# A row transform folded twice, a new order of steps, and norm steps kept in accumulator columns

## The chip, the core and the metric

The kernel runs on one core of one Trainium2 chip. The metric is the device time of one execution in microseconds (us), as the median of several runs. The core has a matrix engine (TensorE, PE in the rows), a vector engine (VectorE, DVE), a scalar engine (ScalarE, ACT), GpSimd (POOL) and a DMA queue on SyncE (SP). Results of TensorE land in PSUM, everything else lies in SBUF.

## The reference

Three parts in a row: a decayed linear attention over blocks, a mixer that adds the real part of a two-dimensional Fourier transform and then a normalised feed-forward block, and a gated convolution with two projections.

```python
def _moe_ref(x, w_ch1, w_ch2):            # x: (2, 768, 512), the attention's output
    X = np.fft.fft(x, axis=1)             # over the 768 rows
    X = np.fft.fft(X, axis=2)             # over the 512 features
    u = x + np.real(X)
    mu = np.mean(u, axis=-1, keepdims=True)
    var = np.mean((u - mu) ** 2, axis=-1, keepdims=True)
    un = (u - mu) / np.sqrt(var + 1e-06)
    return u + np.maximum(un @ w_ch1, 0.0) @ w_ch2      # 512 -> 2048 -> 512
```

Ahead of it, for 8 heads of 64 features and blocks of rows: `intra = (q k^T * decay) v`, `inter = (q * power) state`, and the state is decayed and gets `k^T v`. Behind it: `gate = sigmoid(causal 5-tap convolution of x)`, `out = (gate * (x w_val)) w_out`.

## The kernel before, in words

**Layout.** Everything between attention and output is held transposed: U of each batch is 128 partitions x 4 feature tiles x 768 rows. The features are ordered so that tiles 2 and 3 hold the mirror of tiles 0 and 1, so that a transform can work on sums and differences of tiles.

**Attention.** Twelve chunks of 128 rows (two batches of six). Names of its steps in the order table: L loads a chunk, S the scores (L242), s the masked scores on VectorE (L248), A scores times values (L257), T and t the state update (L295, L303), E the state's share (L268), Kq the scaled query (L216), Y the state's decay, k the scaled keys on ScalarE (L228), a, e and r the copies into U.

**Transform, per batch.** fft_pm (Xm, L311) makes sums and differences of the feature tiles, 768 wide. fft_fold (Xo, L322) folds row s with row 768 - s, plus for the cosine half (w = 0) and minus for the sine half (w = 1), so 384 rows remain; row 384 is taken apart in fft_a384 (XA, L337). First step, fft_D (XD, L350): the folded rows are the stationary side, in three blocks of 128 rows, and the feature tables `cd` are streamed, 257 or 256 columns; fft_Dev (Xd, L359) copies the result to AB. Second step, fft_P and fft_Q (L375, L365): a group of three matmuls, AB blocks against the row tables `cos` and `sin`, 385 columns each, one group for each half of the features (g). An fp32 matmul stands as two records in the trace, so a group has six. fft_qev (Xq) and fft_pc (Xc, L381) evict, fft_mp (Xp, L385) adds and subtracts cosine and sine results, u_add (Xu, L500) adds that to U. fft_P256 (XK, L401) and fft_fix (XF) do feature frequency 256 in two half-array tiles.

**Norm.** ln_mean (Nm, L521) sums U over features with matmuls; ln_center (Nc, L528) subtracts; ln_square and ln_var give the variance in a PSUM tile; ln_newton (Nw, L557 to L566) makes 1/sqrt with eight tiny VectorE operations of 3 columns, in an SBUF tile `var`.

**Feed-forward.** Four blocks of 384 rows, 16 hidden chunks each. F is the first matmul (L627 in block 0, eight records a chunk; L619 to L621 in the others), f and h the relu and its remainder, G the second matmul, U/u and V/v the split of weights into two parts, on ScalarE and then on VectorE or GpSimd. Weights come as 64-bit numbers, in units of 1024 KB, and are converted by bit operations: Da, Dx on ScalarE, Db (L472), Dc (L481), De (L485) on VectorE. Three raw buffers are shared by the units, so a load waits for the conversion three units back.

**What sets the order.** A hand-written table, ORDER: 1454 tokens, run through once. Each engine gets its instructions in the order of the tokens and works through them one by one. A `+` behind a token puts it on VectorE instead of GpSimd (or ScalarE). PSUM tiles of the transform, the norms and the gate share one pool of two buffers.

## Time and profile before

| | |
|---|---|
| median of 3 runs | 447.0 us (445.47 to 447.66) |
| profiled execution | 447.84 us, span 446.1 us |
| TensorE busy | 436.8 us (98%), 2750 records |
| VectorE busy | 314.8 us (71%) |
| ScalarE busy | 248.4 us (56%) |
| GpSimd busy | 114.8 us (26%) |
| DMA | 38.88 MB, most of it in the first 170 us |

The span is what the profiler saw between first and last instruction; the execution's own time is 1.7 us longer. A busy matrix engine is not one at its peak, since records overlap: what counts is the distance from one record's start to the next.

### The profile page before, as it was taken

What the parts mean: (1) busy time and instruction counts of PE and PEld (TensorE: products, weight loads), DVE (VectorE), ACT (ScalarE), POOL (GpSimd) and SP (SyncE); (2) the same over time, 40 slices, a digit from 0 to 9 for tenths busy, and PEclk for the clock granted to TensorE, in tenths of its full rate; (3) what the DMA queues carried; (4) which work ended last, traced back from release to release, by engine and by line L of the source; (5) the groups of instructions that cost most, each with busy time, mean ns of one, the idle gap of its engine ahead of it and who ended that gap; (6) DMA issues with size and microseconds to landing.
All of it is one profiled execution on the core that took longest, in us unless ns stands there. A gap on an engine that the chain in (4) does not pass through costs nothing.

```text
span 446.1 us, 7062 instructions
## 1 busy us (share of the span) xinstructions
PE 436.8 (98%) x2750; PEld 391.9 (88%) x2750; DVE 314.8 (71%) x519; ACT 248.4 (56%) x507; POOL 114.8 (26%) x102
## 2 busy tenths in 40 slices
PE   8999998999999999999999999999999999999996
PEld 6888765876777789999999999999999999999995
DVE  5878997999898989978863677525726883330494
ACT  5576772777667765785436466434635743341442
POOL 2221251021343012136027142122233032331210
PEclk9999998999999999999999999999999999999999
DMA  7899922338634530000000000000000010000101
GB/s 267 301 312 392 396 96 94 101 150 281 225 116 167 168 118 1 1 1 1 0 1 24 0 1 25 0 2 24 0 1 1 24 47 1 0 1 24 49 1 71
DMA packets 14465, 38.88 MB, mean 87 GB/s; under 512 B 1632, under 2 KB 2656, under 8 KB 13408
## 3 DMA queue, kind: packets, MB, share of 16 engines
q1 hardware_dynamic: 14144, 38.04, 23.9%
q8 instruction: 21, 0.34, 0.3%
q10 hardware_dynamic: 288, 0.39, 0.3%
q14 instruction: 12, 0.10, 0.1%
HBM read 35.29 MB, written 3.15 MB: 86 GB/s over the span
## 4 chain that ended last, share of the span: by engine, by line
PE 80%; DVE 3%; ACT 0%; issue 0%
PE acc L619 10%; PE acc L621 10%; PE acc L620 10%; PE ph L627 8%; PE ph L619 8%; PE ph L621 7%; PE ph L620 7%; PE pso L619 4%; PE pso L621 4%; PE pso L620 4%; PE pso L350 1%; PE pso L521 1%; PE pso L550 1%; PE pso L375 1%; PE pso L365 1%; DVE gate L714 1%
## 5 line engine op out<-in xcount | busy, mean ns | idle before, releaser
L619 PE MATMUL acc<-g,w2s 128*128 128x384 f32 x240 | 84.7, 353 | 0.0
L620 PE MATMUL acc<-g,w2s 128*128 128x384 f32 x240 | 80.4, 335 | 0.0
L621 PE MATMUL acc<-g,w2s 128*128 128x384 f32 x240 | 80.4, 335 | 0.0
L648 DVE SCALAR_TENSOR_TENSOR g<-ph,g 128x384 fp32r<-128x384 f32 x60 | 33.0, 553 | 46.1 <-ACT g L643 46.0
L611 ACT CAST w2s<-w 128x512 fp32r<-128x512 f32 x62 | 37.9, 618 | 43.8 <-PE acc L621 42.3
L615 POOL TENSOR_TENSOR w2s<-w,w2s 128x512 fp32r<-128x512 f32 x21 | 27.6, 1315 | 101.1 <-ACT w2s L611 101.1
L597 ACT CAST w1s<-w 128x512 fp32r<-128x512 f32 x48 | 29.6, 617 | 34.8 <-PE ph L621 30.0
L619 PEld LDWEIGHTS acc<-g,w2s 128*128 128x128 f32 x240 | 45.1, 188 | 2.1 <-issue 0.3
L620 PEld LDWEIGHTS acc<-g,w2s 128*128 128x128 f32 x240 | 45.1, 188 | 1.8
L621 PEld LDWEIGHTS acc<-g,w2s 128*128 128x128 f32 x240 | 45.0, 188 | 0.2
L601 POOL TENSOR_TENSOR w1s<-w,w1s 128x512 fp32r<-128x512 f32 x19 | 26.3, 1382 | 70.9 <-ACT w1s L597 55.1
L627 PE MATMUL ph<-uc,w 128*128 128x384 f32 x128 | 43.5, 487 | 0.0
L619 PE MATMUL ph<-hlA,w1s 128*128 128x384 f32 x128 | 43.4, 339 | 0.1
L643 ACT ACTIVATE g<-ph 128x384 fp32r<-128x384 f32 x60 | 29.0, 487 | 25.9 <-PE ph L621 10.5
L714 DVE SCALAR_TENSOR_TENSOR gate<-u,cw,gate 128x384 f32<-128x384 f32 (+4 forms) x64 | 42.1, 670 | 1.5 <-ACT gate L709 0.9
L620 PE MATMUL ph<-hlA,w1s 128*128 128x384 f32 x128 | 42.8, 335 | 0.0
L621 PE MATMUL ph<-hlA,w1s 128*128 128x384 f32 x128 | 42.8, 334 | 0.0
L615 DVE TENSOR_TENSOR w2s<-w,w2s 128x512 fp32r<-128x512 f32 x41 | 31.7, 774 | 15.2 <-ACT w2s L611 15.1
L627 PEld LDWEIGHTS ph<-uc,w 128*128 128x128 f32 x128 | 23.9, 190 | 14.1 <-DVE uc L528 0.2
L601 DVE TENSOR_TENSOR w1s<-w,w1s 128x512 fp32r<-128x512 f32 x29 | 23.3, 803 | 16.5 <-ACT w1s L597 16.5
L619 PEld LDWEIGHTS ph<-hlA,w1s 128*128 128x128 f32 x128 | 24.0, 188 | 1.7 <-DVE g L648 1.5
L620 PEld LDWEIGHTS ph<-hlA,w1s 128*128 128x128 f32 x128 | 24.0, 188 | 0.1
(209 smaller groups left out, 958.8 us busy)
## 6 DMA issues: line engine op xcount, KB each, us to landing
raw<-in_w_dram SPq DMA_DIRECT2D x16, 1024.0 KB, 5.1
ldqk<-in_qT_dram SPq DMA_DIRECT2D x12, 256.0 KB, 5.3
ldqk<-in_k_dram SPq DMA_DIRECT2D x12, 256.0 KB, 5.4
ldv<-in_v_dram SPq DMA_DIRECT2D x12, 256.0 KB, 5.1
ldkT<-in_kT_dram SPq DMA_DIRECT2D x11, 256.0 KB, 5.5
out_dram<-o SPq DMA_DIRECT2D x10, 256.0 KB, 2.0
raw<-in_wv_dram SPq DMA_DIRECT2D x2, 1024.0 KB, 4.7
raw<-in_wo_dram SPq DMA_DIRECT2D x2, 1024.0 KB, 4.8
```

Source lines behind the costliest of these rows:

```text
L350: nc.tensor.matmul(ps[:, 0:n], F[:, w, a, sl], cd[:, a, o:o + n], start=(a == 0), stop=(a == 1), skip_group_check=True)
L597: self.nc.scalar.copy(w[:, 0], self.raw1(f))
L601: eng.tensor_tensor(w[:, 1], self.raw1(f), w[:, 0].bitcast(F32), op=ALU.subtract)
L611: self.nc.scalar.copy(w[:, 0], self.raw2(f))
L615: eng.tensor_tensor(w[:, 1], self.raw2(f), w[:, 0].bitcast(F32), op=ALU.subtract)
L619: nc.tensor.matmul(out, lh, rh, start=start, stop=False)
L620: nc.tensor.matmul(out, lh, rl, start=False, stop=False)
L621: nc.tensor.matmul(out, ll, rh, start=False, stop=stop)
L627: self.nc.tensor.matmul(ph, self.raw1(f)[:, t], self.uc[k][:, t], start=(t == 0), stop=(t == 3))
L643: self.nc.scalar.activation(g[:, 0], self.ph[(k, f)], AF.Relu)
L648: self.nc.vector.scalar_tensor_tensor(g[:, 1], self.ph[(k, f)], 0.0, g[:, 0].bitcast(F32), op0=ALU.max, op1=ALU.subtract)
L714: self.nc.vector.scalar_tensor_tensor(gp[:, o:TB], x, w, gp[:, o:TB], op0=ALU.mult, op1=ALU.add)
```

## The change

Three edits.

1. The row transform folds a second time. fft_fold now gives five tiles of 385 rows in two operations, fft_fold2 (XG) folds those at row 192: even output rows see one half of 192, odd rows the other. The folded rows take the place of the sums and differences in the `pm` tile, and fft_D reads them there; row 192 is taken apart (fft_a192) instead of row 384. The second step (fft_half) has four matmuls of 193 or 192 columns instead of three of 385, into two regions of the PSUM tile; evictions put even and odd rows back in place. fft_P256 has four pairs of records instead of six. The tables are 4x193 instead of 3x385 a partition. fft_fx is gone.
2. The ORDER table is a new one up to the seventh hidden chunk of the second FFN block; behind that its tokens are the old ones in the old order, with a few moved between VectorE and GpSimd. The four groups of a batch's second step, which stood two and two in batch 0 with attention steps between them, stand in a row there, both cosine groups first. The table's first line was and is:

```diff
-S0,0,0 L0,1 Kl k0,0,0 k0,0,1 k0,1,0 S0,0,1 T0,0 s0,0,0 s0,0,1 S0,1,0 S0,1,1 A0,0 k0,1,1 s0,1,0 t0,0 T0,1 s0,1,1 L0,2 Kq0,2+ A0,1 L0,3 Kq0,1 k0,2,0 Y0,1+ S0,2,0 S0,2,1 s0,2,0 a0,0 s0,2,1 t0,1
...
+Kl k0,0,0 k0,0,1 S0,0,0 L0,1 S0,0,1 s0,0,0 L0,2 s0,0,1 T0,0 S0,1,0 t0,0 k0,1,0 k0,1,1 S0,1,1 s0,1,0 A0,0 T0,1 Kq0,1+ k0,2,0 S0,2,0 L0,3 S0,2,1 s0,1,1 k0,2,1 Y0,1+ A0,1 E0,1 Kq0,2 t0,1 e0,0+
...
```

3. ln_newton keeps its three-column values in free columns of the variance's PSUM tile; only `r0` and `lo` lie in SBUF.

```diff
+QS = S // 4
+QE = QS + 1
...
-        self.cs[w] = self.fft.tile([P, 3, HS + 1], F32, name=nm, tag=nm)
+        self.cs[w] = self.fft.tile([P, 4, QE], F32, name=nm, tag=nm)
...
-    def fft_fold(self, eng, b, w, t):
-        z = self.PM[b]
+    def fft_fold(self, eng, b, w):
+        z = self.PM[b].rearrange("p w t s -> p (w t) s")
         if b not in self.F:
-            self.F[b] = self.fft.tile([P, 2, 2, HS], F32, name="F", tag="F")
-        rev = z[:, :, :, S:HS:-1]
-        eng.tensor_tensor(self.F[b][:, w, t, :], z[:, w, t, 0:HS], rev[:, w, t, :], op=ALU.subtract if w else ALU.add)
-
-    def fft_fx(self, eng, b):
-        z = self.PM[b]
-        eng.tensor_tensor(self.F[b][0:1, 1, 0, :], z[0:1, 1, 0, 0:HS], z[:, :, :, S:HS:-1][0:1, 1, 0, :], op=ALU.add)
-
-    def fft_a384(self, b):
+            self.F[b] = self.fft.tile([P, 5, HS + 1], F32, name="F", tag="F")
+        if w == 0:
+            o, x = self.F[b][:, 0:3], z[:, 0:3]
+        else:
+            o, x = self.F[b][:, 3:5], z[:, 2:4]
+        eng.tensor_tensor(o, x[:, :, 0:HS + 1], x[:, :, S:HS - 1:-1], op=ALU.subtract if w else ALU.add)
+
+    def fft_G(self, b, w):
+        z = self.PM[b][:, w]
+        if w == 0:
+            return z.rearrange("p t s -> p (t s)")[:, 0:1536].rearrange("p (t s) -> p t s", t=3)
+        return z
+
+    def fft_fold2(self, eng, b, w, h):
+        x = self.F[b][:, 0:3] if w == 0 else self.F[b][:, 3:5]
+        G = self.fft_G(b, w)
+        if h == 0:
+            eng.tensor_tensor(G[:, :, 0:QS], x[:, :, 0:QS], x[:, :, HS:QS:-1], op=ALU.subtract if w else ALU.add)
+        elif w == 0:
+            eng.tensor_tensor(G[:, :, QS:HS], x[:, :, QS - 1::-1], x[:, :, QS + 1:HS + 1], op=ALU.subtract)
+        else:
+            eng.tensor_tensor(G[:, :, QS:HS - 1], x[:, :, QS - 1:0:-1], x[:, :, QS + 1:HS], op=ALU.add)
+            eng.tensor_copy(G[:, :, HS - 1:HS], x[:, :, QS:QS + 1])
...
+            x = [(cd[:, a, g * P:(g + 1) * P], F[:, a, QS:QE]) for a in range(2)]
             if g < 2:
-                x.append((self.odd, z[:, 1, 0, HS:HS + 1]))
+                x.append((self.odd, F[:, 2, QS:QE]))
...
-            nc.tensor.matmul(ps[:, 0:n], F[:, w, a, sl], cd[:, a, o:o + n], start=(a == 0), stop=(a == 1), skip_group_check=True)
+            nc.tensor.matmul(ps[:, 0:n], G[:, a, sl], cd[:, a, o:o + n], start=(a == 0), stop=(a == 1), skip_group_check=True)
...
+    def fft_half(self, b, g, q, ps):
+        o = 257 * q + 128 * g
+        for n, j in enumerate((0, 2, 1, 1)):
+            h = n % 2
+            self.nc.tensor.matmul(
+                ps[:, h * QE:HS // 2 + 1 + h * QS], self.AB[b][:, j, o:o + 128], self.cs[q][:, (0, 3, 1, 2)[n], 0:QE - h],
+                start=(n == 0), stop=(n > 1), skip_group_check=True,
+            )
...
-        for j in range(3):
-            self.nc.tensor.matmul(ps[:, 0:HS + 1], self.AB[b][:, j, o:o + 128], self.cs[1][:, j, :], start=(j == 0), stop=(j == 2))
+        self.fft_half(b, g, 1, ps)
...
-        eng(q, self.psQ[(b, g)][:, 0:HS + 1])
+        for h in range(2):
+            eng(q[:, h:HS + 1:2], self.psQ[(b, g)][:, h * QE:QE + h * QS])
...
+    def fft_even(self, pc, E, O, a):
+        for w in range(2):
+            self.nc.scalar.activation(pc[:, 2 * w:HS + 1:4], E[:, w:QE:2], AF.Identity, bias=a[:, w])
+        self.nc.scalar.copy(pc[:, 1:HS + 1:2], O)
...
-        for j in range(3):
-            for x in range(2):
-                self.nc.tensor.matmul(
-                    ps[64 * x:64 * x + 64, 0:HS // 2 + 1 - x], self.AB[b][:, j, 256:320], self.cs[0][:, j, x:HS + 1:2],
-                    start=(j == 0), stop=(j == 2), skip_group_check=True,
-                )
+        for n, j in enumerate((0, 2, 1, 1)):
+            h = n % 2
+            self.nc.tensor.matmul(
+                ps[64 * h:64 * h + 64, 0:QE - h], self.AB[b][:, j, 256:320], self.cs[0][:, (0, 3, 1, 2)[n], 0:QE - h],
+                start=(n < 2), stop=(n > 1), skip_group_check=True,
+            )
...
+        x, y = (self.mp[(b, 0, w)][0:1] for w in range(2))
+        ps = self.p256[b]
+        self.fft_even(x, ps[0:1, 0:QE], ps[64:65, 0:QS], self.a192[b][0:1, :, 2:3])
+        self.nc.scalar.copy(y, x)
...
-        var = self.const.tile([P, 4 * n], F32, name="var", tag="var", bufs=2)
-        v, sd, r0, a = (var[:, n * j:n * j + n] for j in range(4))
+        v, sd, r1, a = (self.psv[k][:, TB + n * j:TB + n * j + n] for j in range(4))
+        r0, lo = (self.const.tile([P, n], F32, name=x, tag=x, bufs=2) for x in ("var", "lo"))
         nc.vector.tensor_scalar_add(v, self.psv[k][:, 0:TB:P], 1e-6)
         nc.scalar.activation(sd, v, AF.Sqrt)
         nc.vector.reciprocal(r0, sd)
         nc.vector.tensor_mul(a, v, r0)
         nc.vector.tensor_mul(a, a, r0)
         nc.vector.tensor_scalar(a, a, -0.5, 1.5, op0=ALU.mult, op1=ALU.add)
-        nc.vector.tensor_mul(r0, r0, a)
+        nc.vector.tensor_mul(r1, a, r0)
         rh = self.const.tile([P, n], F32R, name="rh", tag="rh", bufs=2)
-        nc.vector.tensor_copy(rh, r0)
-        nc.vector.tensor_sub(a, r0, rh.bitcast(F32))
-        self.lnr[k] = (rh.bitcast(F32), a)
+        nc.vector.tensor_copy(rh, r1)
+        nc.vector.tensor_sub(lo, r1, rh.bitcast(F32))
+        self.lnr[k] = (rh.bitcast(F32), lo)
```

Three places in the order. First TensorE, from the end of batch 0's second step to the first FFN matmul; L401 is the middle frequency, L521 the mean, L627 the first FFN matmul. Before:

```order
L401 MATMUL pso_862<-cos,AB 64x193
L401 MATMUL pso_862<-cos,AB 64x192
L257 MATMUL pso<-pa,ldv 64x128 x8
L295 MATMUL psd<-ldv,kd 64x64 x8
L257 MATMUL pso<-pa,ldv 64x128 x8
L521 MATMUL pso_930<-u_126,ones 128x384 x4
L268 MATMUL pso<-qs,st 64x128 x16
L627 MATMUL ph<-uc_937,w_0_671 128x384 x12
```

Of the change; there L429, L546 and L652 are these three, and L259, L270, L297, L244 are A, E, T and S:

```order
L429 MATMUL pso_845<-cos,AB 64x193
L429 MATMUL pso_845<-cos,AB 64x192
L270 MATMUL pso<-qs,st 64x128 x8
L297 MATMUL psd<-ldv,kd 64x64 x8
L259 MATMUL pso<-pa,ldv 64x128 x8
L244 MATMUL psS<-ldqk,ldkT_82 128x128 x8
L270 MATMUL pso<-qs,st 64x128 x8
L546 MATMUL pso_935<-u_126,ones 128x384 x4
L259 MATMUL pso<-pa,ldv 64x128 x8
L270 MATMUL pso<-qs,st 64x128 x8
L652 MATMUL ph<-uc_946,w_0_684 128x384 x12
```

Of the middle frequency's rows (six before, four now) the last two are shown. The last scores stand behind more attention work, and two attention steps that stood ahead of the mean now stand behind it.

Second VectorE, up to the centring that the first FFN matmul reads (L528). Before:

```order
L369 COPY tmp<-pso_812 128x385
L385 TENSOR_TENSOR mp<-tmp 128x385
L500 TENSOR_TENSOR u_126<-u_126,mp 128x385
L385 TENSOR_TENSOR mp<-tmp 128x385
L248 TENSOR_TENSOR pa<-psS,mask 128x512 x2
L481 SCALAR_TENSOR_TENSOR w_0_671<-w_0_671,raw 128x1024
L303 TENSOR_TENSOR st<-psd,tmp 128x256
L500 TENSOR_TENSOR u_126<-u_126,mp 128x385
L216 TENSOR_TENSOR qs<-ldqk,lampow 128x512
L472 TENSOR_SCALAR w_1_928<-w_1_928 128x1024
L485 SCALAR_TENSOR_TENSOR w_0_671<-raw,w_0_671 128x1024
L528 TENSOR_TENSOR uc_937<-u_126,pso_930 128x384 x4
```

Of the change, in two pieces that follow on each other: L413 subtracts and adds cosine and sine results, L525 adds to U, L250 masks scores, L553 centres, L506 and L510 are weight conversion, L313 a fold input of batch 1:

```order
L413 TENSOR_TENSOR mp<-tmp 128x385 x2
L525 TENSOR_TENSOR u_126<-u_126,mp 128x383 x2
L525 TENSOR_TENSOR u_126<-u_126,mp 128x385
L250 TENSOR_TENSOR pa<-psS,mask 128x512
L305 TENSOR_TENSOR st<-psd,tmp 128x256
L525 TENSOR_TENSOR u_126<-u_126,mp 128x385
L250 TENSOR_TENSOR pa<-psS,mask 128x512
L525 TENSOR_TENSOR u_126<-u_126,mp 128x385
L413 TENSOR_TENSOR mp<-tmp 128x385
L525 TENSOR_TENSOR u_126<-u_126,mp 128x383
L287 TENSOR_TENSOR tmp<-st,lampow 128x256
```

```order
L510 SCALAR_TENSOR_TENSOR w_0_684<-raw,w_0_684 128x1024
L305 TENSOR_TENSOR st<-psd,tmp 128x256
L250 TENSOR_TENSOR pa<-psS,mask 128x512 x2
L218 TENSOR_TENSOR qs<-ldqk,lampow 128x512
L313 TENSOR_TENSOR pm<-u_127 128x2x384
L553 TENSOR_TENSOR uc_946<-u_126,pso_935 128x384
L317 COPY pm<-pm 128x2
L553 TENSOR_TENSOR uc_946<-u_126,pso_935 128x384 x2
L497 TENSOR_SCALAR w_1_948<-w_1_948 128x1024
L553 TENSOR_TENSOR uc_946<-u_126,pso_935 128x384
```

The additions to U that the mean needs now stand ahead of the last masked scores; a fold input of batch 1 (L313) and the query's scaling (L218) stand right ahead of the centring, and one conversion pass between its operations.

Third GpSimd, in the same stretch. Before:

```order
L500 TENSOR_TENSOR u_126<-u_126,mp 128x385
L285 TENSOR_TENSOR tmp<-st,lampow 128x256
L500 TENSOR_TENSOR u_126<-u_126,mp 128x383 x2
L311 TENSOR_TENSOR pm<-u_127 128x2x384 x2
L315 COPY pm<-pm 128x2
```

Of the change:

```order
L287 TENSOR_TENSOR tmp<-st,lampow 128x256
L413 TENSOR_TENSOR mp<-tmp 128x385
L525 TENSOR_TENSOR u_126<-u_126,mp 128x385
L313 TENSOR_TENSOR pm<-u_127 128x2x384
L317 COPY pm<-pm 128x2
L640 TENSOR_TENSOR w2s<-w_0_655,w2s 128x512
```

One of the two 768-wide fold inputs (L311, now L313) has gone to VectorE; the addition to U that the mean waits for (L525) now stands on GpSimd, right ahead of the other one.

## Rows read from the trace of the kernel before

**Rows 1.** busy us by stretch: PE, PEld, DVE, ACT, POOL; granted clock, DMA share, GB/s
```profile
5.00:65.00 60.00, 58.82 (x759) 48.40 (x758) 52.93 (x95) 40.55 (x129) 15.73 (x15) 1.00 0.87 319
64.30:73.30 9.00, 6.67 (x43) 3.84 (x41) 8.21 (x10) 3.31 (x5) 3.91 (x3) 0.81 0.19 46
73.30:193.00 119.70, 119.07 (x569) 96.57 (x568) 110.06 (x160) 83.09 (x139) 25.48 (x20) 1.00 0.37 129
193.00:420.00 227.00, 226.87 (x1266) 220.32 (x1265) 126.39 (x224) 110.82 (x217) 65.73 (x53) 1.00 0.03 11
```

**Rows 2.** who TensorE waited for: line, releaser, total us, times, longest
```profile
PE pso L521 <- DVE u L500: 2.3, 1, 2.3
...
PE pso L337 <- DVE pm L311: 0.6, 1, 0.6
```

**Rows 3.** timeline of TensorE at the mean: start us, duration us, line, tiles, records [idle before]
```profile
60.72 1.26 PE L401 MATMUL pso<-cos,AB 128*64 128x193 f32 x12
...
64.39 1.56 PE L521 MATMUL pso<-u,ones 128*128 128x384 f32 x4
68.28 2.86 PE L521 MATMUL pso<-u,ones 128*128 128x384 f32 x4 [2.33 <-DVE u L500]
...
73.30 3.17 PE L627 MATMUL ph<-uc,w 128*128 128x384 f32 x9
```

**Rows 4.** timeline of VectorE in the same stretch
```profile
63.24 2.88 DVE L481 SCALAR_TENSOR_TENSOR w<-w,raw 128x1024 int32<-128x1024 int32 x1
...
66.37 1.86 DVE L500 TENSOR_TENSOR u<-u,mp 128x385 f32<-128x385 f32 x1
...
71.18 1.95 DVE L528 TENSOR_TENSOR uc<-u,pso 128x384 f32<-128x384 f32 x4 [0.62 <-PE pso L521]
```

**Rows 5.** timeline of GpSimd in the same stretch
```profile
63.16 4.65 POOL L311 TENSOR_TENSOR pm<-u 128x768 f32<-128x768 f32 x2
```

**Rows 6.** timeline of TensorE in the transform's second step
```profile
47.85 2.21 PE L365 MATMUL pso<-sin,AB 128*128 128x385 f32 x6
49.91 2.11 PE L375 MATMUL pso<-cos,AB 128*128 128x385 f32 x6
51.94 1.16 PE L242 MATMUL psS<-ldqk,ldkT 64*128 64x128 f32 x16
```

**Rows 7.** timeline of TensorE: 24 records of 128 columns and the record behind them
```profile
85.91 2.84 PE L550 MATMUL pso<-ones,tmp 128*128 128x128 f32 x24
88.51 0.43 PE L619 MATMUL acc<-g,w2s 128*128 128x384 f32 x1
```

**Rows 8.** the page's groups: a weight load of fp32 matmuls (count, busy us, mean ns)
```profile
L627 PEld LDWEIGHTS ph<-uc,w 128*128 128x128 f32 x128 | 23.9, 190 | 14.1 <-DVE uc L528 0.2
```

**Rows 9.** groups of VectorE, shapes apart: out<-in, count, busy us, mean ns
```profile
L481 DVE SCALAR_TENSOR_TENSOR w<-w,raw 128x1024 int32<-128x1024 int32 x16 | 22.1, 1384 | 0.4
...
L248 DVE TENSOR_TENSOR pa<-psS,mask 128x512 f32<-128x512 f32 x24 | 15.7, 683 | 3.3 <-PE psS L242 3.2
...
L322 DVE TENSOR_TENSOR F<-pm 128x384 f32<-128x384 f32 x7 | 3.8, 549 | 0.0
...
L385 DVE TENSOR_TENSOR mp<-tmp 128x385 f32<-128x385 f32 x5 | 3.6, 717 | 0.6 <-ACT tmp L381 0.5
...
L481 DVE SCALAR_TENSOR_TENSOR hlB<-hlB,raw 128x1024 int32<-128x1024 int32 x2 | 2.4, 1212 | 0.0
```

**Rows 10.** groups of ScalarE, shapes apart
```profile
L381 ACT ACTIVATE tmp<-pso,a 128x192 f32<-128x192 f32 x4 | 1.7, 426 | 0.0
```

**Rows 11.** DMA issues: KB each, median us from issue to landing
```profile
sin<-in_sin_dram SPq DMA_DIRECT2D x1, 577.5 KB, 11.7
```

**Rows 12.** timeline of the DMA queue: issue of that load
```profile
33.96 0.45 SPq L182 DMA_DIRECT2D sin<-in_sin_dram  x1
```

**Rows 13.** timeline of VectorE in the first norm's small steps
```profile
91.65 2.80 DVE L560 TENSOR_TENSOR var<-var 128x3 f32<-128x3 f32 x1
94.49 0.16 DVE L561 TENSOR_TENSOR var<-var 128x3 f32<-128x3 f32 x1
```

More of the change, by code (lines that the diff above doesn't have):

```diff
@@ L329, in fft_a384, with fft_a192 @@
+    def fft_a192(self, b):
         nc, f = self.nc, self.fft
-        cd, z = self.cd, self.PM[b]
+        cd, F = self.cd, self.F[b]
         ps = self.ps_o.tile([P, 512], F32, name="pso2", tag="pso2")
         for g in range(3):
-            x = [(cd[:, a, g * P:(g + 1) * P] if g < 2 else cd[:, a, 256:257].to_broadcast([P, P]), z[:, 0, a, HS:HS + 1]) for a in range(2)]
+            x = [(cd[:, a, g * P:(g + 1) * P], F[:, a, QS:QE]) for a in range(2)]
             if g < 2:
-                x.append((self.odd, z[:, 1, 0, HS:HS + 1]))
+                x.append((self.odd, F[:, 2, QS:QE]))
@@ L349, in fft_D @@
         for a in range(2):
[L350 removed]
+            nc.tensor.matmul(ps[:, 0:n], G[:, a, sl], cd[:, a, o:o + n], start=(a == 0), stop=(a == 1), skip_group_check=True)
         if w == 0:
[L352 removed]
+            nc.tensor.matmul(ps[:, 1:256:2], G[:, 2, sl], self.odd[:, 1:2].to_broadcast([P, C]), start=False, stop=True, skip_group_check=True)
     def fft_Dev(self, eng, b, j, w):
@@ L843, in tables @@
     cd = np.concatenate([co, np.sin(ang(d, k[:, :256], DM))], axis=1).reshape(2, P, 513).transpose(1, 0, 2)
-    s = np.arange(HS)[:, None]
-    t = np.arange(HS + 1)[None, :]
-    c = np.cos(ang(s, t, S))
-    c[0] *= 0.5
-    sn = np.sin(ang(s, t, S))
-    sn[:, HS] = 0.0
-    return {"cd": np.ascontiguousarray(cd.astype(np.float32)), "cos": c.astype(np.float32), "sin": sn.astype(np.float32)}
+    cs = []
+    for fn in (np.cos, np.sin):
+        sn = fn is np.sin
+        t = np.arange(0, HS + 1, 2)[None, :]
+        ev = fn(ang(np.arange(QS)[:, None], t, S))
+        so = np.arange(QS)[::-1].copy()
+        if sn:
+            so[-1] = QS
+        od = np.zeros((QS, QE))
+        od[:, 0:QS] = fn(ang(so[:, None], np.arange(1, HS, 2)[None, :], S))
+        if not sn:
+            ev[0] *= 0.5
+            od[-1] *= 0.5
+        full = np.zeros((4 * P, QE))
+        full[0:QS] = ev
+        full[4 * P - QS:] = od
+        cs.append(full.astype(np.float32))
+    return {"cd": np.ascontiguousarray(cd.astype(np.float32)), "cos": cs[0], "sin": cs[1]}
 def arrange(q, k, v, lam, moe_w_ch1, moe_w_ch2, moe2_w_val, moe2_conv_w, moe2_w_out):
```

126 lines of the change are left out of this document (57 added, 69 removed).

## Prediction

> **What bounds the kernel now.** I read the busy table by stretch first, then who TensorE waits for, then the timelines around the one long wait. From 193 to 420 us TensorE is busy 226.87 of 227.00 us, from 73.3 to 193 it is busy 119.07 of 119.70 [rows 1]. So from the first FFN matmul on, the end is TensorE's own work; what is taken from that work comes off the span, and a new wait adds to it. Before 73.3 us there is one place that is otherwise: between 64.3 and 73.3 TensorE does 6.67 us of work in 9.00, at a mean granted clock of 0.81, while VectorE is busy 8.21 [rows 1]. The wait list names it: 2.3 us of the first norm's mean (L521) on VectorE's last addition to U (L500), and further on 0.6 us of L337 on a fold input [rows 2]. The timeline shows both halves of the price: the mean's last four records start 2.33 us late, and they take 2.86 us where the first four took 1.56 [rows 3], 1.3 us more, at the lowered clock. Together 3.6 us are lost there. The reason stands beside it: GpSimd runs two 768-wide fold inputs back to back, 4.65 us [rows 5], and in that time one VectorE conversion takes 2.88 us and the addition that the mean waits for 1.86 [rows 4], where the undisturbed forms take 1.21 and 0.55 [rows 9].
>
> VectorE is the second engine to watch: busy 52.93 of 60.00 us up to 65 and 110.06 of 119.70 in the first FFN block, against 126.39 of 227 later [rows 1].
>
> **TensorE: the cut.** An old second-step group (three matmuls of 385 columns, six records) lasts from 47.85 to 49.91 or from there to 51.94 [rows 6], 0.34 us a record. The new group has four matmuls of 193 or 192 columns, eight records. Is half the columns half the time? A 128-column record costs 2.60/24 = 0.108 us [rows 7], so nothing fixed shows down to there, and 193 columns come to 0.17 us; a group to 1.36 us. Eight groups (cosine and sine, two feature halves, two batches) give 8 x 0.67 = 5.4 us. The group of the middle frequency has twelve records in 1.26 us [rows 3], which run in pairs on two halves of the array; it keeps four pairs of six, at most 0.42 us less per batch. That is 6.2 us at most. If the weight load set the pace instead, 0.190 us each [rows 8], a group would last 1.52 us, eight would give 4.1, and the middle frequency nothing. Bounds 4.1 and 6.2; I take 5.8, near the upper one since rows 7 show records 0.108 apart although each has its own load. Half of it, 2.9, lies in batch 0, before the first FFN matmul, and half in the first FFN block, where TensorE never waits.
>
> The page "TensorE: Matmul & The Clock Gate" of the Trainium skill (The mechanism) says that a weight load overlaps running matmuls only where the row group differs. By that, each record would pay its load too, six times 0.53 against eight times 0.36, and the cut would be 2.4 us instead of 5.4. Rows 6 and 7 speak against it here: 0.34 and 0.108 us a record leave no room for 0.190 more.
>
> First-step matmuls keep their number and columns, with two row folds as their stationary side: no change.
>
> **VectorE, GpSimd, ScalarE: the added work.** From 0.549 us for 384 elements and 0.683 for 512 [rows 9] a two-input VectorE operation costs 1.05 ns an element more. A batch had four folds of 384 and a small one. Now it has folds of 3x385 (1.36 us) and 2x385 (0.95), and second folds of 3x192 twice (0.75 each) and 2x192 (0.55), 4.4 us on VectorE, and a last half on GpSimd, about 1.2 us by half of a 768-wide one [rows 5]. Against 2.7 or 1.6 us of VectorE in the two batches before, that is 4.4 us more in all. Each eviction of a sine or cosine result now comes in pieces of 0.43 us [rows 10], and ScalarE takes several evictions over from VectorE. ScalarE is busy 40.55 of 60 us early [rows 1]: some 7 us more there have cover, unless one of them stands before something urgent. In the first FFN block, counted by the order's rows, VectorE's own work rises by only 0.5 us, since one weight conversion and some evictions have gone elsewhere; GpSimd has some 6 us less, so VectorE is held up less. I cost that block's folds at nothing: 9.6 us of VectorE's idle time cover them [rows 1].
>
> The page "SBUF — State Buffer" of the Trainium skill (Who interferes with whom) says that VectorE with two SBUF inputs and a GpSimd operation that reads SBUF exclude each other for a whole instruction. Rows 4 and 5 agree, and it speaks against folds on both engines.
>
> **The norm's small steps.** L560, three columns wide with both inputs in SBUF, took 2.80 us where the next one took 0.16 [rows 13]. With one input in PSUM I expect 0.16, so 2.6 us of VectorE are freed once (nothing to 2.6); no TensorE record waits there, so I count nothing. The cost: the PSUM buffer of the variance, one of two, is held until the last small step. Before TensorE needs it again, two groups of eight first-FFN records stand in its queue, at 3.17/9 us a record [rows 3] 5.6 us; the steps need some 2. Covered.
>
> **When the first FFN matmul starts.** Up to there TensorE loses 2.9 us of work and could lose 3.6 us of waiting; by TensorE alone it could start at 73.3 - 6.5 = 66.8. VectorE decides how much of that comes. The second step starts at about 48.3 (47.85 in the trace [rows 6], with one state update moved ahead of it). Its four groups now stand in a row; the third, the first sine, ends 3 x 1.36 later, at 52.4, and two evictions of 0.43 bring VectorE's first subtraction to 53.3. From there to the fourth centring VectorE has, by the order's rows: 13 operations of 384 or 385 elements (7.1 us), five of 512 (3.4), three of 256 (1.2), one of 768 (0.95), one conversion pass of 1.21 and one no dearer, and one tiny, 15.1 us. One 768-wide fold input still runs on GpSimd there, and one addition: half of the old disturbance (1.67 + 1.31) is 1.5 us. That gives 53.3 + 15.1 + 1.5 = 69.9, which I take: 3.4 us earlier than 73.3. Without any disturbance it is 68.4; with the whole of it and the two missing us of waiting on evictions, 73.
>
> **The sum.** Start of the first FFN 3.4 earlier, 2.9 for batch 1's transform, 0.6 for the wait at L337: 6.9 us. (That step now reads the first fold. It stands three first-FFN groups behind the start, at some 2.6 us each by 3.17/9 a record [rows 3], 8 us; VectorE needs about 6.2 for two conversion passes, two fold inputs, one relu remainder and the fold. It holds, narrowly.) The profiled execution took 447.84 us for a span of 446.1; it would take 440.9. The median of the runs shown is 0.84 lower, so I predict 440.1.
>
> **DMA.** The queue now has one more 1024 KB load ahead of the two tables, which are smaller by a third. The sine table of 577.5 KB was issued at 33.96 and landed 11.7 us later, at 45.7 [rows 11, 12]; its use began at 47.85 [rows 6], 2.1 us of cover. At 319 GB/s [rows 1] the load adds 3.3 us, and smaller tables give 1.2 back: the cover is about used up. A wait of up to 2 us before the second step is in my range, not in my sum.
>
> **Rivals.** (a) TensorE's limit: no wait is left before the first FFN, which starts at 66.8. Then 6.5 + 2.9 + 0.6 = 10.0, time 437.0. For it: the additions that the mean needs now stand ahead of the large GpSimd fold. Against: VectorE's 15 us above. 0.15. (b) The wait moves instead of going: the order puts GpSimd's 768-wide operation and the addition of the last part of U on one queue, right where the query scaling and another fold input on VectorE stand before the four centrings. If that holds VectorE as before, the first FFN starts at 73 and only 0.3 + 2.9 + 0.6 = 3.8 remain: 443.2; with the late table also 445. 0.20 for 442.5 to 444.8. (c) The weight loads set the pace, or even lie bare, so that the cut is 2.4 to 4.1: up to 1.7 us less in the block, 441.8 with the early part as forecast; 0.04. (d) Slower: VectorE is the bound. If its idle time (7.1 us up to 65, 9.6 in the FFN block [rows 1]) is all waiting for results that a shorter TensorE doesn't bring earlier, its added work adds to the time: about 2.5 us before the first FFN and 0.5 in the block, 450.0. It decides from the point where less than 3 us of that idle time can be used. Against: early idle time is spent waiting for TensorE's scores, and the folds need none of them. 0.06. (e) The gain is eaten without being overturned, for instance by rival (b) and waits of one or two us in the first FFN block, at operands that arrive late there: within 0.5% of before, 444.8 to 449.2: 0.10.
>
> **Chances and range.** The forecast (438.5 to 442.5) has 0.45, (a) 0.15, (b) 0.20, (c) 0.04, (d) 0.06, (e) 0.10. About 0.5%, 2.2 us, is what a measurement of this kernel can tell from no change. Faster by more: 0.84; within: 0.10; slower by more: 0.06. The range 435.5 to 445.0 takes in the upper bound of the cut with all waits gone, those of 1.2 us before 65 too [rows 1], and the moved wait with the late table.
>
> **What would show it.** Right: second-step groups of eight records in 1.3 to 1.4 us; the first FFN record at 68.4 to 72 with a granted clock near 1.00 in the 9 us ahead of it; no TensorE wait on VectorE over 1 us behind it; 119.7 us from the first FFN record to the same chunk of the second block shrunk by about 3.3. Wrong: records of 0.19 us (weight loads); a wait of L546 or of the first FFN on VectorE beside a long GpSimd L313; waits of first-FFN or second-FFN records on L640 or L673, which would be VectorE as the bound.

## The result: faster by 1.2%, by two halves that came out otherwise than forecast

| | before | after |
|---|---|---|
| median of 4 runs each, same chip | 447.33 us (445.47 to 448.81) | 441.6 us (441.09 to 441.91) |
| ratio after / before | | 0.9877, 95% interval 0.9853 to 0.9902 |
| span of the profiled execution | 446.1 us | 439.2 us |
| first FFN matmul starts | 73.30 [rows 3] | 68.45 |
| from there to the third chunk of the second FFN block | 119.49 us (192.79) | 117.44 us (185.89) |
| from there to the end of the span | 253.3 us | 253.3 us |

The span lost 6.9 us, as the forecast's sum had it; the median lost 5.7. Of the span's loss, 4.85 us went ahead of the first FFN matmul, 2.05 in the block behind it, nothing later. The forecast had 3.4 and 3.5. Of 52 executions of the kernel before that ran beside the experiments, 18 have a mean granted clock of 0.998 or more and spans of 442.9 to 445.4 us and 34 a clock of 0.996 or less and 444.7 to 447.8 us, as has the profiled one, while all four of the changed kernel have 0.999 or more and 439.1 to 439.2 us.

The busy table by stretch of the changed kernel answers to [rows 1] (columns as there: length, then PE, PEld, DVE, ACT, POOL busy with records, granted clock, DMA share, GB/s):

```profile
59.50:68.50 9.00, 9.00 (x117) 6.68 (x113) 8.97 (x16) 8.08 (x18) 3.98 (x3) 1.00 0.37 135
68.45:186.10 117.65, 116.73 (x573) 96.91 (x572) 111.86 (x164) 82.79 (x144) 24.76 (x18) 1.00 0.37 126
186.10:413.00 226.90, 226.45 (x1265) 220.03 (x1264) 124.67 (x221) 110.41 (x216) 63.39 (x53) 1.00 0.03 11
```

In the 9 us ahead of the first FFN matmul TensorE is busy throughout, at a granted clock of 1.00 (the 2.4 GHz level); before it was 6.67 us at a mean of 0.81. But VectorE is busy there for 8.97 of 9.00 us too: two engines are full at once. TensorE's timeline in that place (start us, duration us, line, tiles, records) answers to [rows 3, 6]:

```profile
50.76 2.78 PE L383 MATMUL pso<-cos,AB 128*128 128x193 f32 x16
53.43 2.88 PE L383 MATMUL pso<-sin,AB 128*128 128x193 f32 x16
56.24 1.16 PE L244 MATMUL psS<-ldqk,ldkT 64*128 64x128 f32 x16
...
58.25 0.82 PE L429 MATMUL pso<-cos,AB 128*64 128x193 f32 x8
59.01 1.09 PE L270 MATMUL pso<-qs,st 64*64 64x128 f32 x16
...
63.63 2.85 PE L546 MATMUL pso<-u,ones 128*128 128x384 f32 x8
...
68.45 8.02 PE L652 MATMUL ph<-uc,w 128*128 128x384 f32 x24
76.31 0.61 PE L355 MATMUL pso<-F,cd 128*128 128x128 f32 x4
```

No row has an idle time in brackets: the mean (L546) neither waits nor slows, and the part of the step that reads the first fold (L355, before L337) comes in time. Two second-step groups take 2.67 us from start to start and the next two 2.81, 1.37 a group.

The chain of work that ended last shows what the totals hide. Of the changed kernel between 58 and 100 us (start us, length us, what):

```profile
63.57 1.20 DVE pa L250 x2
64.77 1.68 DVE qs L218
...
69.84 1.14 DVE w L506
...
91.50 2.30 DVE w L510
...
94.41 0.48 DVE g L673
94.93 2.85 PE ph L652 x8
```

From 63.57 to 94.93 nearly the whole chain is VectorE: masked scores, the query's scaling, weight conversion, folds, a relu remainder. Only at its end does TensorE wait, 0.32 us. So TensorE is kept busy by a VectorE that has nothing left over. The list of TensorE's waits in the changed kernel (line, releaser: us in total, times, longest), against [rows 2]:

```profile
PE ph L644 <- DVE g L673: 1.0, 3, 0.5
PE pso L259 <- ACT kd L230: 0.7, 1, 0.7
PE pso L259 <- ACT u L282: 0.7, 1, 0.7
PE ph L652 <- DVE g L673: 0.3, 1, 0.3
```

(The list's 1.3 us at the very start, which both kernels have, and 0.3 us on a load are left out.) The long wait at the mean is gone; six short ones, on relu remainders and on what ScalarE does for attention, are there.

### The profile page after: what moved, and what is told of

It reads as the page before. It is cut to its first block, busy times and chain, and to the rows that moved or that the text cites. A ratio compares the mean times of both kernels' runs of the same rounds, so it can differ in the third digit from the quotient of the medians.

```text
span 439.2 us, 7095 instructions
## 1 busy us (share of the span) xinstructions
PE 431.0 (98%) x2758; PEld 391.9 (89%) x2758; DVE 312.5 (71%) x518; ACT 252.2 (57%) x524; POOL 109.5 (25%) x98
## 4 chain that ended last, share of the span: by engine, by line
PE 73%; DVE 10%; issue 1%; ACT 1%; DVEq 0%; ACTq 0%
PE acc L646 10%; PE acc L644 10%; PE acc L645 10%; PE ph L644 7%; PE ph L646 7%; PE ph L645 7%; PE ph L652 7%; PE pso L645 4%; PE pso L644 4%; PE pso L646 4%; DVE w L510 1%; PE pso L383 1%; DVE w L506 1%; DVE g L673 1%; DVE w L497 1%
## 5 line engine op out<-in xcount | busy, mean ns | idle before, releaser
L644 PE MATMUL acc<-g,w2s 128*128 128x384 f32 x240 | 85.1, 355 | 0.0
L640 POOL TENSOR_TENSOR w2s<-w,w2s 128x512 fp32r<-128x512 f32 x24 | 33.1, 1382 | 144.4 <-ACT w2s L636 136.0
L644 PEld LDWEIGHTS acc<-g,w2s 128*128 128x128 f32 x240 | 45.1, 188 | 2.1 <-issue 0.3
L644 PE MATMUL ph<-hlA,w1s 128*128 128x384 f32 x128 | 43.4, 339 | 1.0 <-DVE g L673 1.0
L652 PE MATMUL ph<-uc,w 128*128 128x384 f32 x128 | 43.7, 488 | 0.4 <-DVE g L673 0.3
L739 DVE SCALAR_TENSOR_TENSOR gate<-u,cw,gate 128x384 f32<-128x384 f32 (+4 forms) x64 | 40.7, 650 | 2.2 <-ACT gate L734 1.4
L626 DVE TENSOR_TENSOR w1s<-w,w1s 128x512 fp32r<-128x512 f32 x35 | 27.4, 782 | 16.6 <-ACT w1s L622 16.3
L652 PEld LDWEIGHTS ph<-uc,w 128*128 128x128 f32 x128 | 23.7, 190 | 14.7 <-DVE g L673 1.3
L640 DVE TENSOR_TENSOR w2s<-w,w2s 128x512 fp32r<-128x512 f32 x38 | 28.3, 748 | 8.7 <-ACT w2s L636 8.4
L644 PEld LDWEIGHTS ph<-hlA,w1s 128*128 128x128 f32 x128 | 24.0, 188 | 2.3 <-DVE g L673 2.2
L626 POOL TENSOR_TENSOR w1s<-w,w1s 128x512 fp32r<-128x512 f32 x13 | 17.1, 1314 | 29.1 <-ACT w1s L622 29.1
```

What stands on the lines that cost most here:

```text
L626: eng.tensor_tensor(w[:, 1], self.raw1(f), w[:, 0].bitcast(F32), op=ALU.subtract)
L640: eng.tensor_tensor(w[:, 1], self.raw2(f), w[:, 0].bitcast(F32), op=ALU.subtract)
L644: nc.tensor.matmul(out, lh, rh, start=start, stop=False)
L652: self.nc.tensor.matmul(ph, self.raw1(f)[:, t], self.uc[k][:, t], start=(t == 0), stop=(t == 3))
L739: self.nc.vector.scalar_tensor_tensor(gp[:, o:TB], x, w, gp[:, o:TB], op0=ALU.mult, op1=ALU.add)
```

## The experiments

Ratios are to the kernel before, from executions that ran together with it; the changed kernel has 0.9877. Where a run is set against the changed kernel, the difference of the ratios is taken, and 0.001 is 0.45 us. Such a difference is uncertain by more than 1 us, so the spans, which vary less in most of these kernels, stand beside it; the changed kernel's is 439.2.

### The parts alone: norm, order, fold

**Norm alone.** The kernel before with only the third edit.

```diff
-        var = self.const.tile([P, 4 * n], F32, name="var", tag="var", bufs=2)
-        v, sd, r0, a = (var[:, n * j:n * j + n] for j in range(4))
+        v, sd, r1, a = (self.psv[k][:, TB + n * j:TB + n * j + n] for j in range(4))
+        r0, lo = (self.const.tile([P, n], F32, name=x, tag=x, bufs=2) for x in ("var", "lo"))
```

> The kernel before with the norm edit alone: the small steps keep their three-column values in free columns of the variance's PSUM tile. Theory (2.6 us of VectorE are freed, no TensorE record waits there): the three-column product of 2.80 us falls to about 0.16, the time stays within 1 us of before. Rival (VectorE sets the pace of the first FFN block): 2 us or more faster.

Measured: 447.38 us, ratio 0.9999 (0.9983 to 1.0015). VectorE's timeline shows the step of [rows 13] where it took 2.80 us:

```profile
91.30 0.17 DVE L560 TENSOR_TENSOR pso<-pso,var 128x3 f32<-128x3 f32 x1
```

The theory held: the hold is gone and nobody waited for it.

**The old norm steps in the changed kernel**, the same edit backwards.

> The changed kernel with the old norm steps, in an SBUF tile. Theory: the small steps take up to 2.6 us more of VectorE at whichever of them meets a GpSimd operation, no TensorE record waits for it, 0 to 0.5 us slower than the changed kernel. Rival (the steps' time or the longer hold of the PSUM buffer counts): 1 us or more either way.

Measured: 442.54 us, ratio 0.9903 (0.9884 to 0.9921), 1.2 us above the changed kernel. The intervals overlap, so the size rests on the spans (440.6 to 440.8 in all four executions, 1.4 or more longer) and on the trace: there is a wait that the changed kernel doesn't have, and it stands at the second norm, not at the first. The timeline of this kernel at that place, VectorE, GpSimd, TensorE:

```profile
185.22 1.26 DVE L587 TENSOR_SCALAR var<-var 128x3 f32<-128x3 f32 x1
...
185.17 1.29 POOL L626 TENSOR_TENSOR w1s<-w,w1s 128x512 fp32r<-128x512 f32 x1 [1.91 <-ACT w1s L622]
...
187.60 0.44 PE L644 MATMUL ph<-hlA,w1s 128*128 128x384 f32 x1 [1.02 <-DVE g L673]
```

A three-column step lasts as long as the GpSimd operation beside it, the relu remainder behind it is late, TensorE waits 1.02 us. In the changed kernel the same step takes 0.17 us at 185.18 beside the same operation, and TensorE doesn't wait. So the edit is worth nothing in the old order and about 1 us in the new one. The theory fell (0 to 0.5, no TensorE record waits), and its rival held: behind the second norm a record does wait.

**Fold alone.** The second fold in the old order, with the old norm steps.

```diff
-Xo0,0,0+ ... Xo0,0,1+ ... Xo0,1,0+ ... Xx0+ ... Xo0,1,1+
+Xo0,0+ ... Xo0,1+ ... XG0,0,0+ XG0,0,1+ ... XG0,1,0+ XG0,1,1
```

> The second fold without the new order: the old table, with the new folds where the old ones stood, and the old norm steps. Theory (batch 1's cut of 2.9 us counts in full, that of batch 0 vanishes in the wait of the mean, which VectorE sets): 2.5 to 4 us faster than before, 443.5 to 445, and the mean (here still on VectorE's last addition to U, beside GpSimd's two 768-wide operations) waits longer than the 2.3 us of before, about 4 to 5. Rival 1 (the cut counts wherever it lies): 5.9 us faster, 441.5. Rival 2 (the added folds hold VectorE as long as the cut saves): no change, 447.

Measured: 452.54 us, ratio 1.0131 (1.0108 to 1.0153): 5.9 us slower than before. No expectation had this sign. TensorE's waits of this kernel:

```profile
PE pso L354 <- DVE F L326: 3.8, 2, 2.7
PE pso L258 <- ACT mp L403: 2.6, 1, 2.6
PE pso L545 <- DVE u L524: 2.3, 1, 2.3
PE pso L258 <- issue: 1.6, 1, 1.6
PE acc L645 <- DVE w2s L639: 1.3, 1, 1.3
```

The mean's wait stays at 2.3 [rows 2], and the one on "issue" stands where before had 1.05. New are 3.8 us on the first fold (1.09 in batch 0 at 38.19, 2.73 in batch 1 at 87.60), 2.6 us on ScalarE's eviction of the middle frequency, which itself stands waiting 1.37 us for one of VectorE's additions to U, and 1.3 us on a weight remainder behind VectorE's folds. The clock follows: 0.72 from 70 to 76 us, 0.80 from 84 to 90. The first FFN matmul starts at 75.29, 2 us later than before, and the block behind it takes 123.55 us, 4.1 more, although TensorE has 3 us less to do in each.

**Order alone.** The new table with the old, once folded transform and the old norm steps.

```diff
-Xo0,0+ ... Xo0,1+ ... XG0,0,0+ ... XG0,1,0+ ... XG0,1,1
+Xo0,0,0+ Xo0,0,1+ ... Xo0,1,0+ Xx0+ Xo0,1,1+
```

> The new order alone: the kernel before (folded once, old norm steps) with the new table, the second folds left out of it and the four old folds and the row-0 step where the two new ones stand. Theory (in the new order TensorE is bound around the first FFN matmul, so the 5.9 us of TensorE that the second fold takes off count there in full, less what fewer VectorE and ScalarE operations give back): 4 to 5.5 us slower than the changed kernel, 0 to 1.5 us faster than before. Rival 1 (the order gives the gain by itself, the fold is paid for by its own added operations): 1.5 us slower than the changed kernel or less. Rival 2 (the new order only fits the new transform): slower than before.

(The edit is shown against the changed kernel's table.) Measured: 447.16 us, ratio 0.9987 (0.9978 to 0.9997), 0.6 us under before and 5 above the changed kernel: the theory held by the ratios; by the spans (444.9 to 445.4 in ten executions) it is 5.7 to 6.2 above. All ten have a clock of 0.998 or more. The two executions of before at that clock beside them had spans of 444.6 and 444.7, so the order alone wins no more over before than the lowered clock of the others. The first FFN matmul starts at 70.41, 2.9 us earlier than in before's trace, and the mean doesn't wait. The block behind it takes 119.40 us, 0.1 less than before although the wait of L337 is gone: two relu remainders are late in it. It gives back 1.8 behind the third chunk of the second FFN block, where TensorE waits for two more remainders, 1.02 us at the second norm, as with the old steps above, and 0.50 at the fourth. The two in the block:

```profile
172.32 0.44 PE L619 MATMUL ph<-hlA,w1s 128*128 128x384 f32 x1 [0.20 <-DVE g L648]
...
181.23 0.45 PE L619 MATMUL ph<-hlA,w1s 128*128 128x384 f32 x1 [0.31 <-DVE g L648]
```

The chain of this kernel in the same place, ahead of the first FFN matmul, is TensorE's:

```profile
65.65 2.78 PE pso L521 x8
68.43 1.02 PE pso L257 x16
69.46 1.02 PE pso L268 x16
70.48 7.94 PE ph L627 x24
```

The four cases with the old norm steps:

| | old order | new order |
|---|---|---|
| folded once | 1 | 0.9987 |
| folded twice | 1.0131 | 0.9903 |

The fold costs 1.3% in the old order and gives 0.8% in the new one (1% by the spans, 444.9 to 445.4 against 440.6 to 440.8). It exchanges TensorE work for VectorE and ScalarE work, and of these two orders only the one that has room for that work at the right places gets anything for it. In the old order one placement of the folds was tried; a better one isn't excluded.

### Was VectorE held by GpSimd at the mean?

The kernel before with one token changed.

```diff
-Xm1,0,0
+Xm1,0,0+
```

> The kernel before with one operation moved from GpSimd to VectorE in the same place of the order: the first of the two 768-wide fold inputs that ran beside the mean's last addition. Nothing of the fold is in it. Theory (GpSimd's two operations held VectorE, and TensorE lost 2.3 us of waiting and 1.3 of lowered clock by it): VectorE gets 0.8 us more work and loses some 2.5 us of being held; the mean waits under 1 us and 2 to 3.5 us come off. Rival (VectorE is simply late there, whoever runs beside it): the mean waits as long or longer, 0 to 1 us slower.

Measured: 444.8 us, ratio 0.9943 (0.9919 to 0.9967), 2.5 us faster. The timeline of this kernel, with the addition that the mean waits for, the GpSimd operation that is left, and the mean's last four records:

```profile
66.74 0.54 DVE L499 TENSOR_TENSOR u<-u,mp 128x385 f32<-128x385 f32 x1
...
63.58 1.82 POOL L310 TENSOR_TENSOR pm<-u 128x768 f32<-128x768 f32 x1
...
67.34 1.56 PE L520 MATMUL pso<-u,ones 128*128 128x384 f32 x4 [0.97 <-DVE u L499]
```

Against [rows 3, 4]: the addition takes 0.54 us instead of 1.86, the wait is 0.97 instead of 2.33, and the four records take 1.56 again, at full clock. VectorE does more work here and is done sooner: the held engine and the wait are as the prediction read them. The lowered clock doesn't always follow that wait. Norm alone, which left the mean as it was, shows the same wait in its trace, and the records behind it at full clock (TensorE's timeline, then the busy table's row, columns as in [rows 1]):

```profile
65.75 1.56 PE L521 MATMUL pso<-u,ones 128*128 128x384 f32 x4
69.61 1.56 PE L521 MATMUL pso<-u,ones 128*128 128x384 f32 x4 [2.30 <-DVE u L500]
```

```profile
64.30:73.30 9.00, 6.70 (x71) 4.57 (x66) 9.00 (x11) 4.61 (x8) 5.24 (x4) 1.00 0.06 11
```

So of the 3.6 us the 2.3 of waiting stand in both traces, and the 1.3 of the lowered clock (0.81 in before's trace) only in one of them. All five executions of the kernel with one token changed have a clock of 0.999 or more.

### Is TensorE the bound?

The second step's four groups of one batch done twice, over the first result; 32 records more.

```diff
-        self.fft_half(b, g, 1, ps)
+        for _ in range(2 if b == 1 else 1):
+            self.fft_half(b, g, 1, ps)
```

> The changed kernel with the second step's four groups of batch 1 (in the first FFN block) done twice, the second time over the first: 32 records more, 5.2 us of TensorE at 0.163 us each. Theory (TensorE is the bound there): 5.2 us slower than the changed kernel, less at most 1 us that fills the short waits. Rival (VectorE or a DMA is the bound there): under 3 us slower.

> The changed kernel with the second step's four groups of batch 0 (ahead of the first FFN matmul) done twice: 5.2 us more of TensorE. Theory (in the changed kernel no wait is left between the second step and the first FFN matmul, and operands come early by 1 to 2 us at most): 3 to 5.2 us slower than the changed kernel. Rival (the first FFN matmul comes when VectorE has centred, and TensorE has slack ahead of it): under 2 us slower.

Measured: batch 1 gives 446.2 us, ratio 0.9995 (0.9971 to 1.002), 5.3 us above the changed kernel (spans 444.3 to 444.8, 5.1 to 5.6 above); batch 0 gives 445.49, ratio 0.9981 (0.9959 to 1.0003), 4.7 above (443.6 to 443.8, 4.4 to 4.6). Both theories held. With batch 0 doubled the first FFN matmul starts at 73.54, 5.1 us later: no slack of TensorE stands ahead of it. A microsecond of TensorE counts in full in the block, and nearly so ahead of it.

### Has VectorE cover?

The clamp of the weight conversion done twice (the second pass changes nothing), in the changed kernel and in the kernel before.

```diff
-        self.nc.vector.tensor_scalar(d, d, 0.0, HUGE, op0=ALU.max, op1=ALU.min)
+        for _ in range(2):
+            self.nc.vector.tensor_scalar(d, d, 0.0, HUGE, op0=ALU.max, op1=ALU.min)
```

> The changed kernel with one pass of the weight conversion, the clamp, done twice on VectorE (the second changes nothing): some 20 units of about 0.6 to 0.8 us, 12 to 16 us more of VectorE up to 175 us, no work of TensorE. Theory (VectorE's idle time is only in part usable: 5.8 us of 117.65 are left in the first FFN block): 5 to 10 us slower than the changed kernel, as waits of TensorE on VectorE. Rival (VectorE has cover for it): under 2 us.

> The kernel before with the same doubled clamp. Theory (VectorE had 9.6 us idle in the first FFN block before, more than after the change): slower by 1 to 4 us less than the changed kernel is by the same work. Rival (VectorE is as near to being the bound in both): the same loss in both, within 1 us.

Measured: 452.89 us, ratio 1.0138 (1.0088 to 1.0188), 11.7 us above the changed kernel; and 458.02, ratio 1.0253 (1.02 to 1.0306), 11.3 above before. The clamps' rows add 14.0 us of VectorE in the one (29.5 against 15.5) and 14.2 in the other (30.0 against 15.8): 0.8 us of time for each. The first expectation was too low, the second (that before has more room) fell; its rival held. The ratios alone, each uncertain by 2.2 us or more, wouldn't part the two; spans at like clock do: 450.9 against 439.2, 11.7 more, and 455.7 against a median of 443.75, 12.0 more. The stretch from 65 to 185 us, from the busy tables of the four kernels:

| busy of 120 us | before | clamp twice | after | clamp twice |
|---|---|---|---|---|
| TensorE | 117.04 | 110.43 | 119.08 | 112.01 |
| VectorE | 110.26 | 114.70 | 114.34 | 118.51 |

One of them as it stands, the changed kernel with the clamp doubled (columns as in [rows 1]):

```profile
65.00:185.00 120.00, 112.01 (x549) 87.82 (x544) 118.51 (x168) 78.94 (x135) 24.50 (x18) 1.00 0.39 132
```

VectorE has 9.7 us idle in the kernel before. Given more to do, it fills only 4.4 of them, while TensorE falls from 117.0 to 110.4: less than half of that idle time was cover.

**The folds themselves twice**, on VectorE, batch 1 only: the term that the prediction set to nothing.

```diff
-        eng.tensor_tensor(o, x[:, :, 0:HS + 1], x[:, :, S:HS - 1:-1], op=ALU.subtract if w else ALU.add)
+        for _ in range(2 if b == 1 and eng is self.nc.vector else 1):
+            eng.tensor_tensor(o, x[:, :, 0:HS + 1], x[:, :, S:HS - 1:-1], op=ALU.subtract if w else ALU.add)
```

(and the same around the second fold)

> The changed kernel with batch 1's folds on VectorE done twice (both first folds and three of the second ones, the second time over the first): some 4.4 us more of VectorE in the first FFN block, ahead of 100 us. Theory, as the prediction put it (VectorE's idle time of 5 to 10 us in that block covers them): under 0.7 us slower than the changed kernel. Rival (as with the doubled clamp, about 0.8 us of time for each us added to VectorE up to the end of the conversion): 3 to 4 us slower.

Measured: 447.33 us, ratio 0.9983 (0.9967 to 1.0), 4.7 us above the changed kernel. The prediction's theory fell, and the rival's 3 to 4 was low, though not beyond the noise. Four executions at a mean clock of 1.00 have spans of 443.9 to 444.2 us, 4.7 to 5.0 above the changed kernel; six at 0.996, the traced one among them, have 445.5 to 445.7. In its trace the folds' rows add not 4.4 but 6.6 us (10.9 against 4.4), since two of the doubled operations are held beside GpSimd (2.04 us where the second pass takes 0.97, and 1.62 where it takes 0.56). So a microsecond added to VectorE here costs some 0.7 at full clock, about as with the clamp. TensorE's waits that are new in it:

```profile
77.22 0.71 PE L357 MATMUL pso<-F,cd 128*128 128x128 f32 x4 [0.88 <-DVE F L328]
86.40 2.85 PE L654 MATMUL ph<-uc,w 128*128 128x384 f32 x8 [1.33 <-DVE g L675]
97.24 2.04 PE L370 MATMUL pso<-cd,pm 128*128 128x256 f32 x4 [2.90 <-DVE pm L341]
```

They are where the chain above said VectorE sets the pace: on the first fold, on a relu remainder, on the second fold.

### Five steps earlier

The short waits of the changed kernel have names, so they can be tried. Five tokens are moved forward, nothing else (parts of four lines of the table).

```diff
-k1,1,0 s1,1,0 r0,5
+r0,5 k1,1,0 s1,1,0
-Db14 Dl6 V0,3 h0,3
+h0,3 Db14 Dl6 V0,3
-Mt0,0,3 f1,4 u1,6+ h1,2 h1,4
+u1,6+ h1,2 Mt0,0,3 f1,4 h1,4
-f3,7 Mk1,3+ Mo1,0 Mt2,1,3 V3,1 Mz2,0 h3,7
+f3,7 h3,7 Mk1,3+ Mo1,0 Mt2,1,3 V3,1 Mz2,0
```

> The changed kernel with five steps put earlier in the order, nothing else: the copy of chunk 5's rows (ScalarE) ahead of the scaled keys of batch 1's second chunk, and four VectorE steps, the relu remainders of chunks 3, 2 and 7 of blocks 0, 1 and 3 and a weight remainder of block 1, each ahead of one operation that nobody waits for. In the changed kernel TensorE waits 0.96 us at 32.85, 0.48 at 94.3, 0.47 at 176.6 and 0.62 at 340.7 for them. Theory (these short waits are what the cut was partly spent on; VectorE is not the bound): all four go, 1.5 to 2.5 us faster than the changed kernel, 439.1 to 440.1 by the ratio to the kernel before (0.982 to 0.984). Rival (the waits come back at the next operand, since VectorE's total is the bound in the first FFN block): under 0.7 us faster.

Measured: 439.03 us, ratio 0.981 (0.9791 to 0.9829), 3 us under the changed kernel by the ratio and 2.2 by the span (437.0); the intervals don't meet. It is faster than both, and the theory (1.5 to 2.5) held by the span. Its first FFN matmul starts at 67.50, and the distance from there to the third chunk of the second block is 116.56 us, 0.9 less than in the changed kernel. TensorE's waits that are left, among the longest:

```profile
PE psS L244 <- DMA ldqk<-in_qT_dram: 0.9, 1, 0.9
PE pso L259 <- ACT kd L230: 0.7, 1, 0.7
PE ph L644 <- DVE g L673: 0.6, 2, 0.4
```

The wait of L259 on u and that of L652 are gone; of L644's three one is left (0.20), and one of 0.43 has come up at 185.18. VectorE has no more room than before: what was won is not VectorE time but its use for what TensorE needs next.

## Why the prediction was right, and where only by two errors that cancel

**The cut of TensorE: right.** A group of 1.36 us was forecast, 1.37 came; 8 x (2.045 - 1.37) = 5.4 us. The middle frequency takes 0.76 from start to start (58.25 to 59.01) where six pairs took 1.09 (60.72 to 61.81 in before's trace). Some 6.0 in all, forecast 5.8. The rival of the weight loads is out: each load still takes 190 ns,

```profile
L383 PEld LDWEIGHTS pso<-cos,AB 128*128 128x128 f32 x32 | 5.3, 190 | 0.3
```

and records start 2.67/16 = 0.167 us apart, so they lie beside the running matmuls, on the same tile of 128 x 128. The Trainium skill, page "TensorE: Matmul & The Clock Gate" (The mechanism), ties that overlap to different row groups in one sentence and allows it for a background weight buffer in another; this case's rows don't agree with the first.

**The wait at the mean: right in cause, in size only for some executions.** The order alone removes it and the one-token run cuts it to 0.97. The lowered clock behind it, 1.3 of the 3.6 us, belongs to the execution that the prediction read; norm alone has the wait without it.

**First FFN matmul at 69.9: it came at 68.45, and three things in the step were off.** The second step began at 50.76, not 48.3. Attention's part of that is 1.2 us up to the transform's first matmul (37.62, before 36.41), with 0.7 on a copy of rows that ScalarE did late (L259 on u in the list above). The rest, 1.1 beside the state update that was counted, comes up in the first step: its groups now stand singly between attention steps and take 0.97 to 1.06 us from start to start, where four in a row took 0.87 each before. What makes the single ones longer wasn't tried. VectorE's first subtraction so came at 55.64, not 53.3. But VectorE's chain was shorter: the fourth centring ended at 69.85, 14.2 us later and not 16.6. The sum had used durations, and operations of 384 elements start 0.47 us apart where each lasts 0.55, which is 1.9 us over 24 operations. VectorE's timeline:

```profile
60.16 0.55 DVE L525 TENSOR_TENSOR u<-u,mp 128x385 f32<-128x385 f32 x1
60.63 0.55 DVE L413 TENSOR_TENSOR mp<-tmp 128x385 f32<-128x385 f32 x1
...
64.69 1.76 DVE L218 TENSOR_TENSOR qs<-ldqk,lampow 128x512 f32<-128x512 f32 x1
...
69.30 0.55 DVE L553 TENSOR_TENSOR uc<-u,pso 128x384 f32<-128x384 f32 x1
```

So the end of the chain was met to 0.05 us by two errors, of 2.3 and 2.4, that cancel. The third error was the only one that showed: the matmul was put behind the fourth centring, but it works through four tiles in turn and starts when the first is there. The disturbance by GpSimd was sized nearly right: the query's scaling takes 1.76 us instead of 0.68, 1.1 us of the 1.5 allowed.

**Minus 3.5 us behind it: 2.05 came, since two terms were too small.** The wait of L337 went, as forecast, and TensorE's cut is there. But relu remainders are late in the block, by 0.48 us at 94.3, 0.36 at 167.8 and 0.47 at 176.6 (the distance from one record to the next over what it is in an undisturbed place). The last two, in TensorE's timeline of the changed kernel:

```profile
168.38 0.44 PE L644 MATMUL ph<-hlA,w1s 128*128 128x384 f32 x1 [0.20 <-DVE g L673]
...
177.28 0.44 PE L644 MATMUL ph<-hlA,w1s 128*128 128x384 f32 x1 [0.31 <-DVE g L673]
```

They stand in the order alone at the same sizes, so they come with the new order and not with the folds, and the sum had no term for them: the order alone shortens the block by 0.1 us (119.49 to 119.40), not by the 0.6 of L337. The fold then takes it from 119.40 to 117.49 (old norm steps in both), 1.9 us for a cut of 3.0 (2.7 in the groups, 0.3 in the middle frequency). So "I cost that block's folds at nothing" failed by about 1 us. Of this, 0.48 is the remainder at 94.3 and 0.26 one at 83.7, neither of which the order alone has; the rest wasn't found. The 9.6 us of idle time that should have covered the folds are an average over 120 us. Up to 95 us VectorE is the chain, and where more was added to it, each microsecond cost 0.7 to 0.8 (folds and clamp done twice). The five moved tokens get 0.9 us back in this block, by using VectorE's time in another order.

**The norm's small steps: right against before, for one of four norms.** Norm alone gives nothing; in the new order the old steps cost 1 us at the second norm.

**DMA: the cover grew.** It was called used up. The sine table was issued at 37.09 and took 10.1 us, until 47.2, and its first use came at 53.43: 6.2 us, against 2.1. The cosine table, which is used first now, was issued at 34.55 and took 11.4, until 45.95, with 4.8 us to its use at 50.76. The step overlooked that the new order has the sine groups last and starts both later.

**Rivals.** (a), TensorE's limit, had the place right: no wait is left ahead of the first FFN matmul, and a longer second step moves it by as much. Its 66.8 was too early by 1.65, with a second step that began 2.5 late. (b) was there in small: the query's scaling beside GpSimd was held 1.1 us, but the mean's additions already stood ahead of it. (d), VectorE as the bound, had 0.06 and 450.0, and is what the fold does in the old order (452.5). Less than half of the idle time that it asked about could be used in the kernel before. That it lost all the same goes with the order, by the four cases above; what the evictions that went to ScalarE do in it wasn't tried.

**The 1.5 us between 440.1 and 441.6.** The sum was made for the span, and the span fell by the 6.9 us. But the profiled execution of the changed kernel took 441.8 us for a span of 439.2, 2.6 us around it where 1.7 were there before; and it lies 0.2 over its median, where the one of before lay 0.84 over the median shown. 0.9 and 0.6 us: the forecast took both as unchanged. The first isn't explained: the changed kernel's four executions have 1.9 to 2.8 us around one span, most others 1.7 to 1.9. And the 6.9 is luck in part, since before's profiled execution had the lowered clock: against those without it (medians of 443.75 to 444.65 us) the changed kernel's span is 4.6 to 5.5 us shorter.

## What to carry to other kernels

An engine's idle time is cover only where it falls; look at the chain in slices of some 30 us, and price a doubtful microsecond by doing a harmless operation twice, with the added time read from the trace and not from the plan. A wait's cost in clock has to be looked for in several executions. An exchange of work between engines and the order that makes room for it are one change: judged apart, both would have been dropped here. Once two engines are full in the same stretch, the next gain is in which operation goes first: five moved tokens gave a third of what the whole change gave, by the spans.
